# Finishing output tiles one by one, folding the last gate into the weights, and running the last accumulators in one stretch each, in a fused S4-convolution and SwiGLU block

## The chip, the cores and the metric

The kernel runs on one core of a Trainium2 chip. Each core has TensorE (PE, matrix multiply, writes only to PSUM banks), VectorE (DVE), ScalarE (ACT) and GpSimd (POOL), and DMA queues fed by the sync engine (SP) and others. Each engine takes its own queue of instructions in order and waits on semaphores for the others. The metric is the device time of one execution in microseconds (us), lower is better.

## The reference

One block of an adaptive-layer-norm network on 2048 tokens of 640 channels. The first half (a layer norm, a diagonal state-space convolution, a gate) leaves the stream `x`; the second half, which is all that the change touches, is:

```
h = layernorm(x) * (1 + cb) + sb              # cb, sb, gb: 640 values each, from c @ w_mod
out = (silu(h @ w1) * (h @ w3)) @ w2          # w1, w3: 640 x 1728; w2: 1728 x 640
x = x + gb * out
```

## The kernel before

All matrix products are made in three passes of a reduced-precision format: an operand is split into a high part (a cast on ScalarE) and a low part (operand minus high part, on VectorE), and each product is high x high, high x low, low x high. The tiles of high and low parts are named `gh`, `gl` (weights), `uh`, `ul` (the other weights, or the hidden values `h`), `xA`, `xB`, `T1` to `T4` (the normalised stream). Each of these pairs has two buffers, a raw weight `rw` has five.

The tokens are cut into four **quarters** of 512, worked in two **pairs** (A and B). A pair goes through three parts:

- A few hidden slices of 128 channels (`simple`) are made plainly (`plain`): for A, then for B, 15 matmuls for each of the two projections.
- The other slices (`rest`) go through `seven`, a Strassen-like scheme that makes A and B together with seven products in place of eight. It needs differences of the two quarters, `T1` to `T4`, made by `x_sums` (differences, two on VectorE and two on GpSimd) and `x_sum_split` (split in high and low). Each block of `seven` is 54 matmuls. It takes one PSUM bank of the three of `psG` for `b1` and one for `b4`.
- `outputs` multiplies the hidden values by `w2` and adds to the stream. It takes the 14 slices for quarter A (`c` is 0) and then for quarter B (`c` is 1), 28 steps `n`, 15 matmuls each: accumulators `acc[0]` to `acc[3]` hold 128 tokens by 512 channels, `acc[4]` holds the last 128 channels of all 512 tokens transposed. `operands(n + 1)` splits the next step's weight and hidden slice.

When a quarter's 14 steps are over, ScalarE scales `acc[4]` by the gate into `ob`, VectorE multiplies each `acc[k]` by the gate row `gbr` into `gated[k]`, four PE transposes (`tail`, into one bank of `psG`) turn `ob` back, VectorE adds the four transposed pieces and the four gated pieces to the stream tiles `xr`, and four DMAs (`x_out`) store them. For three of the four quarters this is `rest_of`, done in one go after the next step (or, at the change of pairs, after the next pair's plain slices); for the last quarter it is done as the accumulators end.

While pair 0 is in `outputs`, `prepare` makes the stream of pair 1 as side work of the steps: loads, layer norm, transposes (`turn_a`, `turn_b`), then `x_sums` and `x_sum_split` of the tiles in steps 21 to 27.

The order on each engine is the program's order inside `outputs` (it sets `in_order`); elsewhere a scheduler orders the instructions, and `tc.issue_after(ins)` (and `behind(...)`, which wraps it for several instructions) keeps what is written in it behind `ins` on the engine of `ins`. Through a helper, nearly every operation from here on has line L102 in the profile, so tiles tell them apart.

Of the kernel before, what the change touches and what calls it, by code (L numbers as in the profile page):

```python
# [13 lines left out]
OP = mybir.AluOpType  # L14
# [3 lines left out]
P = 128  # L18
# [12 lines left out]
NFT = 14  # L31
# [76 lines left out]
def tile_kernel(ctx: ExitStack, tc: tile.TileContext, a):  # L108
# [780 lines left out]
    def bank(g):  # L889
        return psG.tile([P, 512], F32, name="ps", tag="g") if g else psA.tile([P, 512], F32, name="ps", tag="acc")  # L890

    def room(i):

        return wq.tile([P, 512], F32, name=f"s{i}")
# [327 lines left out]
    def x_out(j, x):  # L1222
        SQ.dma_start(a["out"][j * P:(j + 1) * P, :], x)

    def outputs(q0, order, hs, side, last):


        seq = [(c, f) for c in range(2) for f in order]
        n_all, raws, ops, xr, accs, late = len(seq), {}, {}, [], [], []

        def load(n):
            if n < n_all:
                raws[n] = weight(seq[n][1], "w2")

        def operands(n):
            if n < n_all:
                c, f = seq[n]
                ops[n] = out_operands(raws.pop(n), hs[c][f], f)

        def tail(q, ob, x):  # L1240

            pt = bank(1)
            for i in range(4):
                PE.transpose(pt[:, i * P:(i + 1) * P], ob[:, i * P:(i + 1) * P], ident)
            for i in range(4):
                V.tensor_tensor(x[i][:, 512:], pt[:, i * P:(i + 1) * P], x[i][:, 512:], op=OP.add)

        in_order[0] = True
        for n in range(5):
            load(n)  # L1250
        operands(0)
        in_order[0] = False
        yield
        in_order[0] = True
        for n, (c, f) in enumerate(seq):
            q, pos = q0 + c, n % NFT
            operands(n + 1)
            load(n + 5)
            if pos == 10:
                xr = [x_tile(), x_tile()] + ([x_tile(), x_tile()] if c or last else [x_place("T41"), x_place("T31")])  # L1260
                for i in range(4):
                    SQ.dma_start(xr[i], xs[4 * q + i])
            if pos == 0:
                acc = {k: bank(0) for k in (4, 0, 1, 2, 3)}
            side(n)
            terms = ops.pop(n)

            if c and last and pos == NFT - 2:
                held = terms
                continue  # L1270
            if c and last and pos == NFT - 1:
                terms = held + terms
            if pos == NFT - 1:
                if last or c == 0:
                    gated = [room(4 + i) for i in range(4)]
                else:
                    gated = places(3) + places(3)[:1]
            for k in (4, 0, 1, 2, 3):
                for i, (hh, w) in enumerate(terms):
                    lhs, rhs = (hh[:, k * P:(k + 1) * P], w[:, :512]) if k < 4 else (w[:, 512:], hh)  # L1280
                    PE.matmul(acc[k], lhs, rhs, start=(pos == 0 and i == 0),
                              stop=(pos == NFT - 1 and i == len(terms) - 1))
                if pos < NFT - 1:
                    continue

                if k == 4:
                    ob = room(8)
                    S.activation(ob, acc[4], AF.Copy, scale=modT[:, 2, 4:5])
                    continue
                V.tensor_tensor(gated[k], acc[k], gbr, op=OP.mult)  # L1290
                if c == 0 or not last:
                    continue
                if k == 0:
                    tail(q, ob, xr)
                V.tensor_tensor(xr[k][:, :512], gated[k], xr[k][:, :512], op=OP.add)
                x_out(4 * q + k, xr[k])
            for t in late:
                t()
            late = []
            if pos == NFT - 1 and not (c and last):  # L1300
                def rest_of(q=q, ob=ob, x=xr, gated=gated):
                    tail(q, ob, x)
                    for i in range(4):
                        V.tensor_tensor(x[i][:, :512], gated[i], x[i][:, :512], op=OP.add)
                        x_out(4 * q + i, x[i])
                late.append(rest_of)
        side(n_all)
        in_order[0] = False
        yield
        for t in late:  # L1310
            t()

    def prepare(q0, g):


        steps, got, tiles = {}, {}, ([], [])

        def at(n, fn):
            steps.setdefault(n, []).append(fn)

        mids = (3, 5, 7, 9, 11, 13, 15, 17)
        for i, n in enumerate(mids):
            at(n + 2, lambda i=i: x_norm(4 * q0 + i, got[i], tiles[i // 4], got[i][0]))
        both = []

        def get(i, place):
            if i < 4:
                x = x_next[i]
            elif i < 6:
                x = x_place(("T40", "T21")[i - 4])  # L1330
            else:
                both.extend(places(1) if i == 6 else ())
                x = both[0][:, i - 6]
            got[i] = x_get(4 * q0 + i, x, i < 4, z_place(place) if place else None)

        for i, (n, place) in enumerate(((0, "xB23"), (1, "T120"), (3, "xA01"), (5, "xA23"), (6, "xB23"), (8, "T120"),
                                        (10, None), (12, None))):
            at(n, lambda i=i, place=place: get(i, place))
        for k, n in enumerate((12, 12, 14, 14, 16)):
            at(n, lambda k=k: turn_a(q0, tiles[0], k, g))  # L1340
        for k, n in zip((4, 0, 2, 3, 1), (20, 20, 21, 22, 23)):
            at(n, lambda k=k: turn_b(q0 + 1, tiles[1], k, g))
        for i, n in enumerate(mids):
            at(n, lambda i=i: x_mid(4 * q0 + i, got[i], g))
        for n, i, p in ((21, 0, 0), (22, 0, 1), (23, 0, 2), (24, 0, 3), (24, 1, 0), (24, 1, 1), (25, 1, 2), (26, 1, 3)):
            at(n, lambda i=i, p=p: x_sums(i, (p,)))
        for n, i, name in ((22, 0, "T1"), (24, 0, "T2"), (26, 1, "T1")):
            at(n, lambda i=i, name=name: x_sum_split(i, (name,)))
        at(24, lambda: fetch(NFT - 1, "wg"))
        at(26, lambda: first_block.append(blocks(0)))  # L1350
        at(27, lambda: first_plain.append(plain_weights(NFT - 1)))
        at(27, lambda: x_sum_split(1, ("T2",)))
        at(27, lambda: w_sums(first_block[0], range(4)))
        at(28, lambda: w_split(first_block[0], (1, 0, 2, 3)))

        def side(n):
            for fn in steps.get(n, ()):
                fn()
        return side

    def places(n):

        t = tz.tile([P, SD, 3, NA], F32, name="A").rearrange("p k s b -> p (k s b)")
        if n == 1:
            return [t[:, :2 * D].rearrange("p (i d) -> p i d", i=2)]
        return [t[:, i * 512:(i + 1) * 512] for i in range(3)]

    last_f = NFT - 1
    output = iter(())
    x_next, first_block, first_plain = [], [], []  # L1370
    for pair in range(2):
# [40 lines left out]
        for n, f in enumerate(simple[::-1]):  # L1412
            hB[f] = h_tile()
            ws = ws or plain_weights(f)
            plain("B", f, hB[f], ws)
            ws = None
            if pair == 0 and n < 2:
                x_sums(n)
                x_sum_split(n)
        for i in range(2):  # L1420
            x_late(i)
        if pair:
            for i in range(2):
                x_sum_split(i, ("T4",))
        next(output, None)
        free = []
        order = rest[:10] + ([0, last_f, 1, 2] if pair == 0 else [last_f] + rest[10:])
        output = outputs(q0, order, (hA, hB), prepare(q0 + 2, 1) if pair == 0 else lambda n: None, pair == 1)
        if first_block:
# [8 lines left out]
        for n, f in enumerate(rest):  # L1438
            nxt = block_split(blocks(rest[n + 1])) if n + 1 < len(rest) else None
            if n < 12:  # L1440
                free = free or places(3)
                hA[f] = free.pop(0)
            else:
                hA[f] = h_tile()
            hB[f] = h_tile()
            if pair == 0 and n == len(rest) - 4:
                x_next += [x_tile() for _ in range(4)]
                with tc.issue_after(loaded[0].ins):
                    for i in range(4):
                        SQ.dma_start(x_next[i], a["x"][(8 + i) * P:(9 + i) * P, :])  # L1450
            if nxt is None:
                next(output)
            end = seven(W, hA[f], hB[f], nxt)
            W = nxt
        next(output)
    next(output, None)
# [51 lines left out]
```

## Time and profile before

| | us |
|---|---|
| median of three runs (lowest, highest) | 996.03 (994.35, 996.17) |
| profiled execution, its own time | 997.93 |
| span of the profiled execution, first to last instruction | 995.3 |
| PE busy in the span | 922.2 |
| VectorE, ScalarE, GpSimd busy | 698.1, 541.2, 266.7 |

The second half of the block takes the span from about 427 us on. The profiled execution is 1.9 us above the median of the runs. A row of the profile's timeline gives the start, the time, the engine, the line, the operation, the tile written and the tiles read, the sizes, the number of instructions merged, and in brackets how long the engine was idle ahead of it and who released it.

### The profile page before, as it was taken

How to read it: one execution, taken by the hardware profiler on the slowest of the kernel's cores; microseconds unless marked ns; L12 is line 12 of the kernel's file. 1: busy time of each engine (PE TensorE's matmuls, PEld its weight loads, DVE VectorE, ACT ScalarE, POOL GpSimd, SP SyncE). 2: the span in 40 equal slices, each digit the busy share in tenths (PEclk: the TensorE clock that was granted, in tenths of full speed). 3: DMA queues.
4: the chain of work that ended last, by engine and by line, in shares of the span. 5: the costliest groups of instructions: out<-in, count | busy, mean ns of one | idle time of the engine just before them, and what ended most of it. 6: DMA issues, size and time to landing. Idle time of an engine off the chain costs nothing.

```text
span 995.3 us, 20571 instructions
## 1 busy us (share of the span) xinstructions
PE 922.2 (93%) x8214; PEld 689.2 (69%) x8214; DVE 698.1 (70%) x1243; ACT 541.2 (54%) x793; POOL 266.7 (27%) x274
## 2 busy tenths in 40 slices
PE   5898797998988889799999999999989999999997
PEld 2545354666666666467888888777768888888876
DVE  5598856888898886667666665577876666654545
ACT  3658665899999973246433333365633333333432
POOL 1553333544444530214422210111422222200000
PEclk9855777999999999899999999999989999999999
DMA  9463586554566687785313113995431111213452
GB/s 272 158 228 114 200 198 188 150 150 121 148 161 155 166 211 226 222 183 216 93 54 106 54 53 93 240 263 172 133 119 53 54 54 54 55 38 93 145 165 100
DMA packets 103571, 140.74 MB, mean 141 GB/s; under 512 B 20564, under 2 KB 62676, under 8 KB 103476
## 3 DMA queue, kind: packets, MB, share of 16 engines
q1 hardware_dynamic: 99668, 129.34, 45.2%
q0 software_dynamic: 2304, 7.74, 2.3%
q10 hardware_dynamic: 1504, 2.36, 0.9%
q8 instruction: 64, 1.05, 0.5%
q14 instruction: 31, 0.25, 0.1%
HBM read 107.94 MB, written 31.46 MB: 140 GB/s over the span
## 4 chain that ended last, share of the span: by engine, by line
PE 66%; ACT 14%; DVE 10%; DMA 3%; issue 3%; POOL 2%; SPq 1%; ACTq 0%; POOLq 0%; DVEq 0%
PE ps L102 51%; ACT cs L135 4%; ACT A L135 3%; ACT ph L135 3%; PE p L570 2%; PE pa L432 2%; ACT L135 2%; PE pq L444 2%; PE pt L539 1%; POOL ph L472 1%; PE pm L299 1%; DMA zs<-zt 1%; PE pu L406 1%; PE pk L521 1%; PE pz L612 1%
## 5 line engine op out<-in xcount | busy, mean ns | idle before, releaser
L102 DVE TENSOR_TENSOR s<-ps,s 128x512 f32<-128x512 f32 x138 | 94.8, 688 | 86.3 <-PE ps L102 84.5
L472 POOL TENSOR_TENSOR ph<-thi,iota 128x1024 int32<-128x1024 int32 x40 | 85.5, 2136 | 175.1 <-DVE A L508 78.2
L102 DVE TENSOR_TENSOR gl<-rw,gh 128x640 fp32r<-128x640 f32 x87 | 77.7, 893 | 72.3 <-ACT gh L102 72.3
L102 ACT CAST gh<-rw 128x640 fp32r<-128x640 f32 x87 | 63.3, 727 | 103.8 <-PE ps L102 87.9
L102 PE MATMUL ps<-xA,gh 128*128 128x512 f32 x280 | 89.0, 397 | 4.4 <-DVE h L102 4.1
L570 PE MATMUL p<-uk,s 128*64 128x256 f32 x640 | 79.1, 389 | 14.0 <-PE pa L432 5.6
L102 PE MATMUL ps<-gh,uh 128*128 128x512 f32 x224 | 87.5, 391 | 0.0
L102 PE MATMUL ps<-gl,uh 128*128 128x512 f32 x224 | 87.2, 389 | 0.0
L102 POOL TENSOR_TENSOR S<-rw 128x256 f32<-128x256 f32 x46 | 37.0, 806 | 180.3 <-DVE S0l L102 148.0
L102 PE MATMUL ps<-gh,ul 128*128 128x512 f32 x208 | 81.1, 390 | 0.0
L570 PEld LDWEIGHTS p<-uk,s 128*64 128x64 f32 x640 | 45.2, 138 | 39.3 <-PE pa L432 8.4
L102 PEld LDWEIGHTS ps<-xA,gh 128*128 128x128 f32 x280 | 53.3, 191 | 17.6 <-DVE h L102 4.5
L102 PE MATMUL ps<-xA,gl 128*128 128x512 f32 x140 | 55.2, 394 | 0.0
L135 ACT ACTIVATE A<-pa 128x1024 f32<-128x1024 f32 x40 | 40.4, 1024 | 25.7 <-PE pa L432 24.4
L497 DVE TENSOR_TENSOR E<-A,cs 128x1024 f32<-128x1024 f32 x40 | 51.1, 1277 | 1.7 <-ACT A L135 1.7
L504 DVE TENSOR_TENSOR A<-A,ph 128x1024 f32<-128x1024 f32 x40 | 50.2, 1255 | 0.0
L102 ACT ACTIVATE s<-ps 128x512 f32<-128x512 f32 (+1 forms) x33 | 19.7, 597 | 54.1 <-PE ps L102 49.3
L612 PE MATMUL pz<-Y,i 64*128 64x128 f32 x640 | 45.1, 285 | 4.1 <-issue 2.8
L612 PEld LDWEIGHTS pz<-Y,i 64*128 64x128 f32 x640 | 38.9, 189 | 13.9 <-issue 11.2
L102 PEld LDWEIGHTS ps<-gl,uh 128*128 128x128 f32 x224 | 42.1, 188 | 9.0
L102 PEld LDWEIGHTS ps<-gh,uh 128*128 128x128 f32 x224 | 42.1, 188 | 8.7
L539 PE MATMUL pt<-s,K 128*64 128x128 f32 x640 | 47.3, 291 | 0.5 <-ACT uk L138 0.5
(259 smaller groups left out, 2332.8 us busy)
## 6 DMA issues: line engine op xcount, KB each, us to landing
rw<-in_w_dram SPq DMA_DIRECT2D x52, 320.0 KB
us<-u SPq DMA_DIRECT2D x16, 640.0 KB
s<-in_s_dram SPq DMA_DIRECT2D x40, 256.0 KB
i<-in_i_dram SPq DMA_DIRECT2D x40, 256.0 KB
rw<-in_wg_dram SPq DMA_DIRECT2D x31, 320.0 KB
rw<-in_wu_dram SPq DMA_DIRECT2D x28, 320.0 KB
uk<-us SPq DMA_DIRECT2D x32, 256.0 KB
zs<-zt SPq DMA_DIRECT2D x32, 256.0 KB
```

The source lines that it names most:

```text
L102: ins = fn(*args, **kw)
L135: return tc.keep_in_program_order(S.activation(*args, **kw))
L299: PE.matmul(pm[g, :n], scb[:, k], w[:, k, :], start=(k < 4), stop=(k > 0), tile_position=(0, g.start))
L406: PE.matmul(pu[h][hh * 64:hh * 64 + 64, q, :320], s1r[r], x[r, hh * 320:hh * 320 + 320], start=not (one and h == 0), stop=True, tile_posit ...
L432: keep(PE.matmul(pA[s][:, rr, :], w[r, ch, :], r2[r, js, :].rearrange("p j b -> p (j b)"), start=st, stop=not st, tile_position=(r.start, 0)))
L444: keep(PE.matmul(pQ[s][:, rr, :256], w[r, ch, :], rv, start=(i == 0), stop=(i == 3), tile_position=(r.start, 0)))
L472: hold(G.tensor_tensor(p, bc(thi[:, sl], 2, NPH), bc(iota, 1, SD), op=OP.mult))
L497: keep(V.tensor_tensor(EC[s][:, :, 1:3, :], AA[s][:, :, 1:3, :], mid(cs[s]), op=OP.mult))
L504: keep(V.tensor_tensor(A[:, :, 1:3, :], A[:, :, 1:3, :], mid(ph[s]), op=OP.mult))
L539: keep(PE.matmul(pt[c * 64:c * 64 + 64, g, :], kk[:, g, :], s1[:, c, :], start=True, stop=True, tile_position=(0, c * 64)))
L570: keep(PE.matmul(p2[par * 64:par * 64 + 64, pi, c, :], s2[:, pi * 2 + par, c * 64:c * 64 + 64], uk[:, 0:kn + 1:kn, f, :], start=True, stop ...
L612: ins = keep(PE.matmul(pz[:, par, (g % 2) * 2 + pi, :], i1[r, pi, c, :], Y[r, pi, c, :], start=(c == 0), stop=(c == 1), tile_position=(par ...
```

## The change

1. **Tile by tile.** `rest_of` is replaced by four steps `finish`, one for each tile of 128 tokens: one PE transpose into a bank of its own, the add of the transposed piece, the add of the gated piece, the store. Inside `outputs` two are done after each of the next two steps. At the change of pairs they are done one each behind blocks 1 to 4 of the next pair's `seven`, through `before` (the old generator, which now yields after each), and `ob` moves from `room(8)`, which `plain` also uses, to one of the `places`.
2. **Last gate in the weights.** In the last quarter `gate` multiplies the first 512 columns of each of its 14 raw `w2` tiles by `gbr` on VectorE, two steps ahead of their split. The four gate multiplies at the end fall away, and the accumulators are added to the stream straight from PSUM.
3. **Last accumulators in one run each.** Of the last two steps only `acc[2]` and `acc[3]` are held back; the step before the last runs `acc[4]`, `acc[0]`, `acc[1]` with its own operands. The four tails come after `acc[1]`, in four banks.
4. **`T2` behind the change of pairs.** The split of `T2` is taken out of steps 24 and 27 and written after the plain slices of pair 1.
5. In pair 0, `x_sums` and `x_sum_split` are put `behind(*turned)`, the last splits of the plain `xA`/`xB` tiles.

```
+        def gate(n):
+
+            if last and NFT <= n < n_all:
+                V.tensor_tensor(raws[n][:, :512], raws[n][:, :512], gbr, op=OP.mult)
+
...
-        def tail(q, ob, x):
-
-            pt = bank(1)
-            for i in range(4):
-                PE.transpose(pt[:, i * P:(i + 1) * P], ob[:, i * P:(i + 1) * P], ident)
-            for i in range(4):
-                V.tensor_tensor(x[i][:, 512:], pt[:, i * P:(i + 1) * P], x[i][:, 512:], op=OP.add)
+        def tail(i, ob, x, g):
+
+            pt = bank(g)
+            PE.transpose(pt[:, :P], ob[:, i * P:(i + 1) * P], ident)
+            V.tensor_tensor(x[i][:, 512:], pt[:, :P], x[i][:, 512:], op=OP.add)
+
+        def finish(i, q, ob, x, gated, g):
+
+            tail(i, ob, x, g)
+            V.tensor_tensor(x[i][:, :512], gated[i], x[i][:, :512], op=OP.add)
+            x_out(4 * q + i, x[i])
...
             operands(n + 1)
             load(n + 5)
+            gate(n + 3)
...
             terms = ops.pop(n)
+            run = [(k, terms) for k in (4, 0, 1, 2, 3)]
 
             if c and last and pos == NFT - 2:
-                held = terms
-                continue
+                held, run = terms, run[:3]
             if c and last and pos == NFT - 1:
-                terms = held + terms
+                run[3:] = [(k, held + terms) for k in (2, 3)]
             if pos == NFT - 1:
-                if last or c == 0:
-                    gated = [room(4 + i) for i in range(4)]
+                if c == 0:
+                    gated, ob = [room(4 + i) for i in range(4)], room(8)
+                elif last:
+                    ob = room(8)
                 else:
-                    gated = places(3) + places(3)[:1]
-            for k in (4, 0, 1, 2, 3):
+                    *gated, ob = places(3) + places(3)[:2]
+            for k, terms in run:
...
-                V.tensor_tensor(gated[k], acc[k], gbr, op=OP.mult)
-                if c == 0 or not last:
-                    continue
-                if k == 0:
-                    tail(q, ob, xr)
-                V.tensor_tensor(xr[k][:, :512], gated[k], xr[k][:, :512], op=OP.add)
-                x_out(4 * q + k, xr[k])
-            for t in late:
+                elif not (c and last):
+                    V.tensor_tensor(gated[k], acc[k], gbr, op=OP.mult)
+                else:
+                    V.tensor_tensor(xr[k][:, :512], acc[k], xr[k][:, :512], op=OP.add)
+                    if k == 1:
+                        for i in range(4):
+                            tail(i, ob, xr, 1)
+                    for i in ((), (0, 1), (2,), (3,))[k]:
+                        x_out(4 * q + i, xr[i])
+            for t in late[:2]:
                 t()
-            late = []
+            late = late[2:]
             if pos == NFT - 1 and not (c and last):
...
+                late = [lambda i=i, t=(q, ob, xr, gated, 1 - c): finish(i, *t) for i in range(4)]
...
-        for n, i, name in ((22, 0, "T1"), (24, 0, "T2"), (26, 1, "T1")):
+        for n, i, name in ((22, 0, "T1"), (26, 1, "T1")):
...
-        at(27, lambda: x_sum_split(1, ("T2",)))
...
             if pair == 0 and n < 2:
-                x_sums(n)
-                x_sum_split(n)
+                with behind(*turned):
+                    x_sums(n)
+                    x_sum_split(n)
+        if pair:
+            for i in range(2):
+                x_sum_split(i, ("T2",))
...
-        next(output, None)
-        free = []
+        before, free = output, []
...
             end = seven(W, hA[f], hB[f], nxt)
+            if 1 <= n <= 4:
+                with behind(end):
+                    next(before, None)
```

How the built programs stand follows at three places. VectorE, ahead of pair 1's plain slices (`T_8157`, `T_8158` are `T1` of the second tile, `T_8183`, `T_8272` its `T2`, `T_8282`, `T_8284` its `T4`; the `gl` is the weight of the plain slice, `A<-ps,gbr` the gate multiplies of the quarter that has just ended). Before:

```order
L102 TENSOR_TENSOR ul<-h,uh 128x512
L102 TENSOR_TENSOR T_8157<-s_7607,T_8157 128x512
L102 TENSOR_TENSOR T_8282<-s_7715,T_8282 128x512
L102 TENSOR_TENSOR gl<-rw,gh 128x640
L102 TENSOR_TENSOR T_8183<-s_8034,T_8183 128x512
L102 TENSOR_TENSOR A<-ps,gbr 128x512 x4
```

The same place, with the change:

```order
L102 TENSOR_TENSOR ul<-h,uh 128x512
L102 TENSOR_TENSOR T_8158<-s_7607,T_8158 128x512
L102 TENSOR_TENSOR T_8272<-s_8037,T_8272 128x512
L102 TENSOR_TENSOR T_8284<-s_7715,T_8284 128x512
L102 TENSOR_TENSOR ul<-rw,uh 128x384
L102 TENSOR_TENSOR gl<-rw,gh 128x640
L102 TENSOR_TENSOR A<-ps,gbr 128x512 x4
```

The split of `T2` and a split of the first block's weight (`ul<-rw,uh 128x384`) now stand ahead of the plain slice's `gl`, where one split stood behind it and the other much later.

VectorE, from there to the first block of `seven` (`xm` are the stream tiles of the quarter that has ended, `h<-ps,s` 64x512 the plain slices' results for A and B, `T_8273`, `T_8276`, `T_8275`, `T_8278` the tiles `T3`, `s_8326` the first sum of the first block). Before:

```order
L102 TENSOR_TENSOR S3l<-S_8198,S3h 128x256
L102 TENSOR_TENSOR xm<-A,xm 128x512 x4
L102 TENSOR_TENSOR gl<-rw,gh 128x640
L102 TENSOR_TENSOR T_8273<-s_7963,T_8273 128x512
L102 TENSOR_TENSOR ul<-rw,uh 128x384 x2
L102 TENSOR_TENSOR xm<-ps,xm 128x128 x3
L102 TENSOR_TENSOR T_8276<-s_8070,T_8276 128x512
L102 TENSOR_TENSOR h<-ps,s_8250 64x512
L102 TENSOR_TENSOR xm<-ps,xm 128x128
L102 TENSOR_TENSOR gl<-rw,gh 128x640
L102 TENSOR_TENSOR h<-ps,s_8270 64x512
```

With the change:

```order
L102 TENSOR_TENSOR S3l<-S_8196,S3h 128x256
L102 TENSOR_TENSOR gl<-rw,gh 128x640
L102 TENSOR_TENSOR ul<-rw,uh 128x384
L102 TENSOR_TENSOR xm<-A,xm 128x512
L102 TENSOR_TENSOR h<-ps,s_8247 64x512
L102 TENSOR_TENSOR xm<-A,xm 128x512 x2
L102 TENSOR_TENSOR T_8275<-s_7966,T_8275 128x512
L102 TENSOR_TENSOR xm<-A,xm 128x512
L102 TENSOR_TENSOR gl<-rw,gh 128x640
L102 TENSOR_TENSOR h<-ps,s_8267 64x512
L102 TENSOR_TENSOR T_8278<-s_8073,T_8278 128x512
L102 TENSOR_TENSOR s_8326<-ps,s_8318 128x512
```

The weight's `gl` and `ul` moved ahead of the stream adds, both `h` moved forward, and the four adds `xm<-ps` are gone from here; the four adds `xm<-A` are still here.

PE, at the end (`ps_10133`, `ps_10134` are `acc[0]`, `acc[1]` before; `ps_10143`, `ps_10144` are `acc[1]`, `acc[2]` with the change; `ident` marks the transposes). Before:

```order
L102 MATMUL ps_10133<-gh_10442,uh_10446 128x512
L102 MATMUL ps_10133<-gl_10443,uh_10446 128x512
L102 MATMUL ps_10133<-gh_10442,ul_10447 128x512
L102 MATMUL ps_10469<-ident_63,s8_10460 128x128 x4
L102 MATMUL ps_10134<-gh_10419,uh_10423 128x512
L102 MATMUL ps_10134<-gl_10420,uh_10423 128x512
L102 MATMUL ps_10134<-gh_10419,ul_10424 128x512
```

With the change:

```order
L102 MATMUL ps_10143<-gh_10464,uh_10468 128x512
L102 MATMUL ps_10143<-gl_10465,uh_10468 128x512
L102 MATMUL ps_10143<-gh_10464,ul_10469 128x512
L102 MATMUL ps_10494<-ident_63,s8_10481 128x128
L102 MATMUL ps_10497<-ident_63,s8_10481 128x128
L102 MATMUL ps_10500<-ident_63,s8_10481 128x128
L102 MATMUL ps_10503<-ident_63,s8_10481 128x128
L102 MATMUL ps_10144<-gh_10441,uh_10445 128x512
L102 MATMUL ps_10144<-gl_10442,uh_10445 128x512
L102 MATMUL ps_10144<-gh_10441,ul_10446 128x512
```

The transposes moved from behind `acc[0]` to behind `acc[1]`, and write four banks of a pool that has three buffers, where they wrote one.

More of the change, by code (lines that the diff above doesn't have):

```diff
@@ L1286, in outputs @@
                 if k == 4:
-                    ob = room(8)
                     S.activation(ob, acc[4], AF.Copy, scale=modT[:, 2, 4:5])
-                    continue
-                V.tensor_tensor(gated[k], acc[k], gbr, op=OP.mult)
-                if c == 0 or not last:
-                    continue
-                if k == 0:
-                    tail(q, ob, xr)
-                V.tensor_tensor(xr[k][:, :512], gated[k], xr[k][:, :512], op=OP.add)
-                x_out(4 * q + k, xr[k])
-            for t in late:
+                elif not (c and last):
[8 more added lines that the diff above has]
+            for t in late[:2]:
                 t()
-            late = []
+            late = late[2:]
             if pos == NFT - 1 and not (c and last):
[L1301 to L1306, printed above, removed]
+                late = [lambda i=i, t=(q, ob, xr, gated, 1 - c): finish(i, *t) for i in range(4)]
         side(n_all)
@@ L1311, in outputs @@
             t()
+            yield
     def prepare(q0, g):
```

## The prediction

> **What bounds the kernel now.** I read the page first, then busy times by stage, then the timeline of each engine wherever PE pauses behind 427 us.
>
> ```profile
> span 995.3 us, 20571 instructions
> 725.00:750.00 25.00, 20.94 (x83) 16.82 (x82) 19.06 (x32) 8.24 (x16) 6.90 (x8) 0.86 0.37 120
> 975.00:1000.00 25.00, 14.89 (x65) 11.35 (x63) 10.45 (x19) 4.44 (x7) 0.00 (x0) 0.89 0.14 53
> ```
>
> A stage row gives the stretch, its length, PE's busy time, then those of the others; the last but two is the granted clock. From 475 to 975 us only this one row in 25 us falls well below 25 us of PE, and it is at the change of pairs, with a lower clock. PE is the bound, so an edit is worth what it takes out of PE's pauses, plus what it takes off the end.
>
> The change of pairs on PE and on VectorE:
>
> ```profile
> 721.10 0.39 PE L102 MATMUL ps<-xA,gl 128*128 128x512 f32 x1
> ...
> 729.97 0.40 PE L102 MATMUL ps<-T,S0h 128*128 128x512 f32 x1
> 734.43 1.22 PE L102 MATMUL ps<-xA,gh 128*128 128x512 f32 x2 [4.06 <-DVE h L102]
> ...
> 740.10 0.63 PE L102 MATMUL ps<-xA,gh 128*128 128x512 f32 x2
> ...
> 747.15 0.62 PE L102 MATMUL ps<-xA,gh 128*128 128x512 f32 x2
> ...
> 748.51 0.62 PE L102 MATMUL ps<-T,S1h 128*128 128x512 f32 x2
> ```
>
> ```profile
> 717.05 2.38 DVE L102 TENSOR_TENSOR T<-s,T 128x512 fp32r<-128x512 f32 x2
> 719.35 1.36 DVE L102 TENSOR_TENSOR gl<-rw,gh 128x640 fp32r<-128x640 f32 x1
> 720.63 1.22 DVE L102 TENSOR_TENSOR T<-s,T 128x512 fp32r<-128x512 f32 x1
> 721.77 2.47 DVE L102 TENSOR_TENSOR A<-ps,gbr 128x512 f32<-128x512 f32 x4
> ...
> 726.05 4.12 DVE L102 TENSOR_TENSOR xm<-A,xm 128x512 f32<-128x512 f32 x4
> 730.10 0.81 DVE L102 TENSOR_TENSOR gl<-rw,gh 128x640 fp32r<-128x640 f32 x1
> ...
> 732.37 0.67 DVE L102 TENSOR_TENSOR xm<-ps,xm 128x128 f32<-128x128 f32 x3
> ...
> 733.68 0.69 DVE L102 TENSOR_TENSOR h<-ps,s 64x512 f32<-64x512 f32 x1
> ```
>
> Six matmuls go from 747.15 to 748.51, so 0.227 each. PE stands still from 730.2 to 734.43 (4.2 us): its next matmul needs a bank that `h` (733.68) frees, and `h` stands behind the stream adds. Then 13 matmuls take 5.67 us (734.43 to 740.10) in place of 2.95: the clock is halved, 2.7 more. With 0.2 of switching to and from the transposes the place costs 7.1 us.
>
> The other pauses:
>
> ```profile
> 467.59 0.39 PE L102 MATMUL ps<-xB,gh 128*128 128x512 f32 x1
> 468.65 0.50 PE L102 MATMUL ps<-xB,gh 128*128 128x512 f32 x1 [0.68 <-DVE xB L102]
> ```
>
> ```profile
> 466.75 1.30 POOL L102 TENSOR_TENSOR s<-s,s 128x512 f32<-128x512 f32 x1 [1.43 <-DVE s L102]
> ```
>
> ```profile
> 467.19 1.40 DVE L102 TENSOR_TENSOR xB<-s,xB 128x512 fp32r<-128x512 f32 x1
> ```
>
> ```profile
> 712.40 0.39 PE L102 MATMUL ps<-uh,gh 128*128 128x512 f32 x1
> 713.54 0.49 PE L102 MATMUL ps<-uh,gl 128*128 128x512 f32 x1 [0.76 <-DVE gl L102]
> 714.15 0.50 PE L102 MATMUL ps<-ul,gh 128*128 128x512 f32 x1
> ```
>
> ```profile
> 707.69 1.32 DVE L102 TENSOR_TENSOR gl<-rw,gh 128x640 fp32r<-128x640 f32 x1 [0.74 <-ACT gh L102]
> ...
> 710.37 2.38 DVE L102 TENSOR_TENSOR T<-s,T 128x512 fp32r<-128x512 f32 x2
> 712.68 0.81 DVE L102 TENSOR_TENSOR gl<-rw,gh 128x640 fp32r<-128x640 f32 x1
> ```
>
> ```profile
> 947.78 0.39 PE L102 MATMUL ps<-uh,gh 128*128 128x512 f32 x1
> 948.62 0.50 PE L102 MATMUL ps<-uh,gl 128*128 128x512 f32 x1 [0.44 <-DVE gl L102]
> 949.22 0.50 PE L102 MATMUL ps<-ul,gh 128*128 128x512 f32 x1
> ```
>
> ```profile
> 982.22 0.39 PE L102 MATMUL ps<-ul,gh 128*128 128x512 f32 x1
> 983.26 0.50 PE L102 MATMUL ps<-uh,gh 128*128 128x512 f32 x1 [0.66 <-ACT uh L102]
> ...
> 985.93 0.60 PE L102 MATMUL ps<-ident,s 128*128 128x128 f32 x4
> ```
>
> Less 0.227 per matmul started, they cost: at 467, 1.06 - 0.23 = 0.8 (0.9 with the slower next); at 712, 1.75 - 0.45 = 1.3; at 947, 1.44 - 0.45 = 1.0; at 982, 10 matmuls take 3.71 in place of 2.27, so 1.4.
>
> **The change, part by part.**
>
> *Change of pairs.* VectorE's queue decides, and it is walked in the new order. An f32 128x512 operation takes 0.60 when nothing runs on GpSimd (2.47 for four) and 1.0 to 1.2 beside it (2.38 for two, 4.12 for four). One `T2` split, 1.2, leaves the queue ahead of 712.68 (it goes ahead of the weight split of 707.69, into its 0.74 of idle time), so the `gl` there comes 1.0 sooner and of the 1.3 at 712 some 0.3 is left. Ahead of the plain `gl` of 719.35 there now stand the other `T2` split (1.2) and a `ul` of 384 columns (estimate 0.8, 384/512 of 1.1). The four `A` adds then start at 721.77 - 1.2 + 0.8 = 721.4, and the plain `gl`, now last ahead of them, ends there; PE wanted it at 721.10 - 1.0 = 720.1 and waits 1.3. Plain A and B end 28 matmuls later, 727.8. The next weight's `gl` stands at the end of the small splits (726.05 - 0.4 = 725.7) and is done at 726.9, in time. With the tails gone, `b1` has the third bank free: no wait where 4.2 us stood. Then `ul` 0.7, one `xm` 1.0, `h` of A at 729.2; ScalarE needs that for B's silu, then copies `b1` at about 730.9, and PE, which wanted to go on with `b1` 12 matmuls after 727.8 (730.5), waits 0.4. VectorE goes on with two `xm`, `T3`, `xm`, `gl`, `h` of B, `T3` and the first sum, eight at 0.6 to 0.7: 734.2, and PE wants that sum at 730.9 + 15 x 0.227 = 734.3. [...] The other 27 matmuls of the block end at 740.5, where before it was 747.15: **-6.6**. Bounds: -7.4, all waits gone; -2.5, if VectorE is 1.4 later and the clock drops again (2.7).
>
> [...]
>
> [...]
>
> *Tails in blocks 1 to 4.* One transpose each, alone between matmuls of 512. A merged row of four takes 0.35 to the next matmul, so one alone is bounded by 0.1 and 0.35; I take 0.25, nearer the top since the switch is paid each time: **+1.0** (0.4 to 1.4). VectorE has room there. Each store now stands in SP's queue between two weight loads and waits for VectorE's add, so the load behind it waits too; in the program's order the first one comes behind the loads for block 5, whose buffers come free only then, and a weight is loaded two blocks (24 us) early: 0.
>
> *First boundary, 671 us.* Here `prepare` takes two banks of the same pool right behind the transposes.
>
> ```profile
> 670.69 0.60 PE L102 MATMUL ps<-ident,s 128*128 128x128 f32 x4
> ```
>
> ```profile
> 671.33 0.49 DVE L102 TENSOR_TENSOR xm<-ps,xm 128x128 f32<-128x128 f32 x2
> ```
>
> With two banks for two tails, its second bank is the first tail's, free when VectorE has added it: 671.33 + 0.3 = 671.65. PE wants it at about 671.05: **+0.5** (0 to 0.9).
>
> *Pair 0, 467 us.* The differences go behind the last `xB` split, so GpSimd's 1.30 no longer lies beside it, and the split ends 0.9 sooner: **-0.9** (-0.95 to 0). The weight split pushed behind them (`gl` for the third plain slice) is wanted some 11 us later than 468.65, and its queue needs about 9. GpSimd's four differences start 4.5 us later, at about 468.5, but without the gaps between them; they end no later than now, and so do the weight sums behind them.
>
> *Third quarter, 947 us.* The `gl` stood behind four stream adds, 0.6 each; two of these now stand a step later, with two of the stores, which hold up SP's next weight load by a step of the five that it is ahead: **-1.0** (-1.1 to -0.3).
>
> *Gate in the weights.* 14 multiplies of 128x512 on VectorE, 0.6 to 0.7 each, 9 us in all, on a VectorE that idles ahead of each weight split:
>
> ```profile
> L102 DVE TENSOR_TENSOR gl<-rw,gh 128x640 fp32r<-128x640 f32 x28 | 23.1, 824 | 43.1 <-ACT gh L102 43.1
> ```
>
> 43.1/28 is 1.5 us per step, and GpSimd is idle: cost 0. If that cover were gone, 0.7 for each step.
>
> *The end.*
>
> ```profile
> 986.12 0.69 DVE L102 TENSOR_TENSOR s<-ps,gbr 128x512 f32<-128x512 f32 x1 [1.98 <-PE ps L102]
> ...
> 991.50 0.69 DVE L102 TENSOR_TENSOR xm<-s,xm 128x512 f32<-128x512 f32 x1
> ```
>
> From the first matmul of the last-but-one step (two ahead of 982.22, 981.76) PE now does 9, then 3, 3, 3 of the last step, with no wait, since the last hidden split is ready at 983.2: `acc[1]` is done at 985.8. Three transposes, then the fourth waits for a bank, so for VectorE: `xr[0]`, `xr[1]` to 986.65, first tail to 986.95. PE goes on at 987.1 with 12 matmuls to 989.8, and the last add (0.4 behind the last matmul's start, as 986.12 is behind its own) runs from 990.05 to 990.75, where it now ends at 992.2. The last store follows as before (995.3 - 992.2 = 3.1): **-1.4**, of which the bank costs 0.8 (bounds -2.3 to -0.7).
>
> Sum: -6.6 + 1.0 + 0.5 - 0.9 - 1.0 - 1.4 = **-8.4 us**. On the profiled execution's 997.93 that is 989.5; it lies 1.9 above the median, as runs of a kernel differ by about that, so on the median 996.03 it gives **987.6**.
>
> **The rivals.**
>
> *VectorE stays late at the change of pairs.* The four adds `xm<-A` still stand there, and two splits more stand ahead of plain A. [...] For it speaks the queue without a gap from 714 to 734; against it, that `h` of A is 4.5 us sooner.
>
> *All waits go.* The fourth transpose and the `gl` of plain A are not waited for (0.8 + 1.3 + 0.4): 985.1. Against it, a pool of three buffers.
>
> *The gate holds VectorE.* Each multiply waits for its weight's load, in order, with `gl` of the next step behind it. VectorE has 1.5 - 0.7 = 0.8 us to spare a step, so a load late by 1.4 us costs 0.6 x 14 = 8.4, all of the gain, and one late by 2.2 gives 1007. Against it: a raw weight has five buffers and is loaded some three steps (10 us) ahead of its gate, and the last store's 3.1 us is the price of one such transfer.
>
> *It does not do what it says.* The scheduler leaves the stream adds in place and PE waits as long: only the end and the quarters pay, 994.2.
>
> **How the numbers follow.** Forecast 0.66, late VectorE 0.16, all waits go 0.08, nothing at the change of pairs 0.06, the gate 0.04. Faster by over 0.2% (2 us, about what a measurement here can tell): 0.66 + 0.16 + 0.08 and a little of the fourth, 0.91; same 0.05; slower 0.04. The range is 985.0 to 991.8: it takes in the forecast's bounds one or two at a time and the first two rivals.
>
> **What would show it.** PE has no pause over 2 us from 720 to 745 and no clock of 0.5 there; a pause of about 1 us on `gl` stands near 720; none near 467 and 947; the fourth transpose at the end waits about 0.8 for VectorE. A halved clock behind 720, or `gh` waiting for VectorE's gate step after step in the last quarter, would make it wrong.

## The result and the profile after

| | before | after |
|---|---|---|
| median of 7 runs of each, us | 996.17 | 991.21 |
| ratio, 95% interval | | 0.9947 (0.9926 to 0.9967) |
| profiled execution: time, span, us | 997.93, 995.3 | 991.21, 989.4 |

The change makes the kernel 5.0 us faster where 8.4 were forecast: the sign was right, the size was not, and the time lies near the upper end of the range that was given, 985.0 to 991.8. Single executions of the changed kernel took from 986.72 to 993.36 us, so the terms are read as lengths of stages within one trace. A stage goes from one PE row to another that both kernels have. Of the executions of the changed kernel that y2 timed, one took 1735.49 us; it is left out of the median given there.

Stage rows of the changed kernel, columns as in the prediction's first fence:

```profile
span 989.4 us, 20588 instructions
475.00:500.00 25.00, 23.62 (x103) 18.95 (x102) 18.03 (x28) 10.72 (x21) 9.81 (x11) 1.00 0.31 93
725.00:750.00 25.00, 24.25 (x107) 19.73 (x106) 20.61 (x34) 9.53 (x18) 6.90 (x8) 1.00 0.24 76
```

From 725 to 750 PE is busy 24.25 us where it was 20.94, and the granted clock is 1.00 where it was 0.86. A stage that was full before, 475 to 500, has lost 1.4 us of PE: a new pause.

The change of pairs on PE, first the row of before that opens it, then the changed kernel:

```profile
703.07 0.38 PE L102 MATMUL ps<-ident,A 128*128 128x128 f32 x2
```

```profile
703.90 0.38 PE L102 MATMUL ps<-ident,A 128*128 128x128 f32 x2
...
721.45 0.61 PE L102 MATMUL ps<-xA,gh 128*128 128x512 f32 x2
723.20 0.50 PE L102 MATMUL ps<-xA,gl 128*128 128x512 f32 x1 [1.13 <-DVE gl L102]
...
732.17 0.39 PE L102 MATMUL ps<-T,S1l 128*128 128x512 f32 x1
733.31 0.74 PE L102 MATMUL ps<-xA,gh 128*128 128x512 f32 x2 [0.75 <-ACT s L102]
...
744.37 0.62 PE L102 MATMUL ps<-T,S1h 128*128 128x512 f32 x2
```

From the last transposes of the output stage to the first `S1h` of the second block it was 748.51 - 703.07 = 45.44 us; now it is 744.37 - 703.90 = 40.47: **-4.97**. Two pauses stand there, 1.30 for the plain `gl` (721.45, two matmuls of 0.227 taken off) and 0.91 for ScalarE's copy of `b1` (732.17). Ahead of them the `gl` at 712 to 715 still costs 0.99, and a new 0.36 stands at 710.7: PE waits there for VectorE's split of a hidden slice (710.48), and the split of `T2` (708.48, behind its cast on ScalarE) now stands ahead of that.

The `gl` at 712 was to come 1.0 sooner. On VectorE and on GpSimd:

```profile
712.41 1.91 DVE L102 TENSOR_TENSOR gl<-rw,gh 128x640 fp32r<-128x640 f32 x1
```

```profile
712.03 1.60 POOL L102 TENSOR_TENSOR s<-s,s 128x512 f32<-128x512 f32 x1 [2.87 <-ACT gh L102]
```

It took 1.91 beside GpSimd's difference, where it took 0.81 before, and so ended 10.42 behind the row that opens the stage (714.32 - 703.90), exactly as before (713.49 - 703.07).

The new pause in pair 0, on PE, then on VectorE, then on GpSimd:

```profile
478.17 0.39 PE L102 MATMUL ps<-T,ul 128*128 128x512 f32 x1
478.80 0.73 PE L102 MATMUL ps<-xB,gh 128*128 128x512 f32 x2 [0.24 <-DVE h L102]
480.67 0.50 PE L102 MATMUL ps<-xB,gl 128*128 128x512 f32 x1 [1.14 <-DVE gl L102]
```

```profile
471.77 1.77 DVE L102 TENSOR_TENSOR s<-s,s 128x512 f32<-128x512 f32 x1
473.46 4.68 DVE L102 TENSOR_TENSOR T<-s,T 128x512 fp32r<-128x512 f32 x4
...
479.27 1.35 DVE L102 TENSOR_TENSOR gl<-rw,gh 128x640 fp32r<-128x640 f32 x1
```

```profile
471.32 1.67 POOL L102 TENSOR_TENSOR s<-s,s 128x512 f32<-128x512 f32 x1 [0.63 <-DVE s L102]
473.62 1.68 POOL L102 TENSOR_TENSOR s<-s,s 128x512 f32<-128x512 f32 x1 [0.63 <-DVE s L102]
```

The pause of 0.94 at 467 is gone; this one costs 0.40 + 1.42 + 0.11 = 1.93.

A tail ahead of the second block and the end, on PE:

```profile
755.25 0.27 PE L102 MATMUL ps<-ident,A 128*128 128x128 f32 x1
755.28 0.71 PE L102 MATMUL ps<-xA,gh 128*128 128x512 f32 x2
755.82 0.39 PE L102 MATMUL ps<-xA,gl 128*128 128x512 f32 x1
```

```profile
981.30 0.49 PE L102 MATMUL ps<-ident,s 128*128 128x128 f32 x3
982.45 0.33 PE L102 MATMUL ps<-ident,s 128*128 128x128 f32 x1 [0.65 <-DVE xm L102]
```

From the tail's transpose to the third matmul behind it is 0.57, for two matmuls of 0.227: 0.12 lost. At the end the fourth transpose follows 1.15 behind the row of three; with 0.057 taken off for each of the three, a quarter of a matmul's 0.227 and so an estimate, 0.98 is lost. The three themselves start 0.11 apart (0.49 for three, 0.27 for one); by that it is 0.82.

| stage | before, us | after, us | forecast | measured |
|---|---|---|---|---|
| pair 0, 459.87 and 459.12 to 666.40 and 666.62 | 206.53 | 207.50 | -0.9 | +0.97 |
| first boundary, from there to 703.07 and 703.90 | 36.67 | 37.28 | +0.5 | +0.61 |
| change of pairs | 45.44 | 40.47 | -6.6 | -4.97 |
| four blocks with tails (12.24 each; 748.51 to 797.47, 744.37 to 793.91) | 48.96 | 49.54 | +1.0 | +0.58 |
| third quarter's tail, from there to 976.10 and 971.44 | 178.63 | 177.53 | -1.0 | -1.10 |
| end, from there to the span's end | 19.2 | 17.96 | -1.4 | -1.24 |

The six sum to -5.15. The two spans differ by 5.9, of which 0.75 lies ahead of 459 us, where the change touches nothing; the medians differ by 5.0. Two terms fail: pair 0 by 1.9 with the wrong sign, and the change of pairs by 1.6.

### The profile page after: what moved, and what is told of

Read it like the earlier page. It is cut to its first block, busy times and chain, and to the rows that moved or that the text cites. A ratio compares the mean times of both kernels' runs of the same rounds, so it can differ in the third digit from the quotient of the medians.

```text
span 989.4 us, 20588 instructions
## 1 busy us (share of the span) xinstructions
PE 918.2 (93%) x8214; PEld 686.2 (69%) x8214; DVE 706.2 (71%) x1253; ACT 540.9 (55%) x793; POOL 265.5 (27%) x274
## 3 DMA queue, kind: packets, MB, share of 16 engines
q8 instruction: 64, 1.05, 0.4%
## 4 chain that ended last, share of the span: by engine, by line
PE 65%; ACT 16%; DVE 10%; DMA 3%; issue 3%; POOL 2%; SPq 0%; ACTq 0%; DVEq 0%; POOLq 0%
PE ps L102 50%; ACT cs L135 4%; ACT A L135 3%; ACT ph L135 3%; PE p L570 2%; PE pa L432 2%; ACT L135 2%; PE pq L444 2%; DMA zs<-zt 2%; PE pt L539 1%; PE pm L299 1%; PE pk L521 1%; PE pz L612 1%; PE pu L406 1%; POOL ph L472 1%
```

## The experiments

Each of x1 to x8 was executed once, with its trace, so their stages are compared and not their whole times. Parts 1 and 3 of the change were not undone by themselves: what they are worth is read from the stages above alone.

### x1 and x2: each wait at the change of pairs by itself

x1 undoes the part on `T2` alone:

```diff
-        for n, i, name in ((22, 0, "T1"), (26, 1, "T1")):
+        for n, i, name in ((22, 0, "T1"), (24, 0, "T2"), (26, 1, "T1")):
...
+        at(27, lambda: x_sum_split(1, ("T2",)))
...
-        if pair:
-            for i in range(2):
-                x_sum_split(i, ("T2",))
```

> Only the part on T2 is undone: its two splits stand in steps 24 and 27 of the output stage again, everything else as in the changed kernel. Theory 1 (the two splits and the 384-column ul ahead of the plain gl are what PE waits for at 721): the plain gl ends 2.2 us sooner, so the pause of 1.30 there is gone (under 0.2), so is the 0.36 at 710.7, where a T2 cast stands ahead of gh on ScalarE, and the pause at 712 to 715 grows from 0.99 back to the 1.3 of before; the second block of the last pair then starts about 1.3 us sooner against the start of the step at 704. Theory 2, that of the prediction (the move is worth 1.0 at 712 and costs nothing else): the block starts 0.3 to 1.0 later, with 1.3 at 712 and some pause still at 721.

```profile
700.96 0.38 PE L102 MATMUL ps<-ident,A 128*128 128x128 f32 x2
...
727.82 0.39 PE L102 MATMUL ps<-T,S1l 128*128 128x512 f32 x1
729.77 0.73 PE L102 MATMUL ps<-xA,gh 128*128 128x512 f32 x2 [1.56 <-ACT s L102]
...
733.77 0.74 PE L102 MATMUL ps<-xB,uh 128*128 128x512 f32 x2 [0.30 <-DVE s L102]
...
741.43 0.61 PE L102 MATMUL ps<-T,S1h 128*128 128x512 f32 x2
```

The waits went as theory 1 has it (none at 721, 0.36 gone at 710, 1.39 at 712), but the stage takes 741.43 - 700.96 = 40.47 us, the same as with the part in. The 1.3 of `gl` came back as 0.8 more for the copy of `b1` and 0.46 for VectorE's sum. Neither theory's number holds: this part of the change is worth nothing in this kernel. With the `T2` split back in its queue the `gl` at 712 ends 10.42 behind the row that opens the stage (711.38 - 700.96), the same as without it.

x2 makes two edits far apart:

```diff
-        sg = room(8)
+        sg = h if last and c == "B" else room(8)
...
-                            tail(i, ob, xr, 1)
+                            tail(i, ob, xr, int(i < 3))
```

> Two edits 250 us apart, read from the trace apart. (a) The silu of plain B of the 64-row slice is written into B's own h tile, so that it needn't wait until VectorE has read A's silu out of the common buffer. If that wait is the cause of the 0.91 at 732 (ScalarE's copy of b1 stands behind the silu, the silu behind h of A), the pause is gone and the second block of the last pair starts 0.9 sooner. If ScalarE is late for another reason, the copy of b1 starts within 0.3 of where it did and the pause stays over 0.5. (b) The fourth transpose at the end takes the bank that acc[4] left, in place of the third bank of the transposes. If the bank is the cause of its wait for VectorE (0.98), the wait is gone and the span ends 0.8 to 1.0 sooner behind the fourth transpose; if VectorE is the bound at the end, the last add starts within 0.3 of where it did against the start of the last step.

```profile
736.43 0.39 PE L102 MATMUL ps<-T,S0l 128*128 128x512 f32 x1
737.58 0.73 PE L102 MATMUL ps<-xB,uh 128*128 128x512 f32 x2 [0.76 <-DVE s L102]
...
982.16 0.60 PE L102 MATMUL ps<-ident,s 128*128 128x128 f32 x4
```

(a) The pause at 732 is gone, and 0.92 stands at 736.43 for VectorE's sum instead; the stage is 40.44. The cause named for the pause was right, its removal bought nothing. (b) The four transposes run in one row, and from there to the end of the span it takes 989.3 - 982.16 = 7.1 us where it was 8.1: the bank was the wait, about 0.9 (spans are given to 0.1).

### x5 to x8: VectorE's queue, and both chains at once

x5 keeps the four `xm<-A` adds out of the change of pairs (a), and puts the gate back on the outputs of the last quarter (b):

```diff
-        V.tensor_tensor(hA, c21, sg, op=OP.mult)
+        vend[0] = V.tensor_tensor(hA, c21, sg, op=OP.mult)
...
-                with behind(end):
+                with behind(end, vend[0]):
                     next(before, None)
...
-                V.tensor_tensor(raws[n][:, :512], raws[n][:, :512], gbr, op=OP.mult)
...
-                    V.tensor_tensor(xr[k][:, :512], acc[k], xr[k][:, :512], op=OP.add)
+                    V.tensor_tensor(gated[k], acc[k], gbr, op=OP.mult)
+                    V.tensor_tensor(xr[k][:, :512], gated[k], xr[k][:, :512], op=OP.add)
```

> Two edits 170 us apart, read apart. (a) The tails of blocks 1 to 4 go behind the last VectorE instruction of their block too, not only behind its last matmul: the four 512-column adds xm<-A that VectorE works off at 729 to 734, in the change of pairs, come behind blocks 1 to 4. Two runs so far moved the waits there (T2 back in the steps; a place of its own for B's silu) and won nothing. Theory 1: VectorE's whole queue from 714 to 737 is the bound. Without the four adds (3.1 us of it) the pauses at 732 and 736 together are under 0.3, the pause of 1.3 at the plain gl stays, since the adds stand behind it, and block 1 starts 0.9 to 1.0 sooner against the step at 704. Theory 2: ScalarE's chain of silu and copy is the bound, the adds only fill gaps: a pause of 0.6 or more stays at 732 to 737. (b) The gate goes back from the weights to the outputs in the last quarter (14 multiplies less in the steps, four more at the end). If the gate in the weights costs nothing, the steps from 907 to 971 take as long as before within 0.2; if it costs, they are shorter. The end is 1.2 to 1.8 later: two more multiplies ahead of the tails, one ahead of the last add.

VectorE in the changed kernel, and then in x5, from the weight splits to the first sum:

```profile
727.34 1.36 DVE L102 TENSOR_TENSOR gl<-rw,gh 128x640 fp32r<-128x640 f32 x1
728.63 1.09 DVE L102 TENSOR_TENSOR ul<-rw,uh 128x384 fp32r<-128x384 f32 x1
729.64 1.22 DVE L102 TENSOR_TENSOR xm<-A,xm 128x512 f32<-128x512 f32 x1
730.89 0.69 DVE L102 TENSOR_TENSOR h<-ps,s 64x512 f32<-64x512 f32 x1
731.51 1.28 DVE L102 TENSOR_TENSOR xm<-A,xm 128x512 f32<-128x512 f32 x2
...
733.31 0.68 DVE L102 TENSOR_TENSOR xm<-A,xm 128x512 f32<-128x512 f32 x1
...
735.97 0.69 DVE L102 TENSOR_TENSOR s<-ps,s 128x512 f32<-128x512 f32 x1
```

```profile
726.95 1.09 DVE L102 TENSOR_TENSOR ul<-rw,uh 128x384 fp32r<-128x384 f32 x1
728.07 0.69 DVE L102 TENSOR_TENSOR h<-ps,s 64x512 f32<-64x512 f32 x1
...
731.34 0.69 DVE L102 TENSOR_TENSOR s<-ps,s 128x512 f32<-128x512 f32 x1
...
734.34 0.69 DVE L102 TENSOR_TENSOR s<-ps,s 128x512 f32<-128x512 f32 x1 [1.98 <-PE ps L102]
```

(a) From `ul` to the first sum it is 7.34 us with the adds, 4.39 without. No pause is left at 732, nor at 736, where x2 had one; 1.3 is left at the plain `gl`, and the stage takes 39.39: 1.08 less, as theory 1 has it. VectorE then even idles 1.98 behind the first sum.

(b) From the first step of the last pair's output stage to the last transposes the changed kernel takes 981.30 - 890.48 = 90.82 us, x5 978.52 - 887.74 = 90.78: the gate in the weights costs nothing. The end is 10.2 long in place of 8.1, 2.1 later, above the 1.2 to 1.8 expected: the fourth transpose alone waits 1.4 more.

x6 is (a) of x5 with x1; x7 adds x2's two edits and takes the differences of pair 0 out of `behind(*turned)`; x8 is x7 without x1's edit.

```diff
-                with behind(*turned):
-                    x_sums(n)
-                    x_sum_split(n)
+                x_sums(n)
+                x_sum_split(n)
```

> The four xm<-A adds behind blocks 1 to 4 as in the run x5, and the T2 splits back in steps 24 and 27 as in x1, gate as in the changed kernel. Theory 1 (VectorE's queue as a whole is the bound, and with 3.1 us out of it the splits find room): no pause over 0.3 at 721, 732 or 736, 1.3 stays at 712; block 1 starts 2.0 to 2.4 sooner than in the changed kernel against the step at 704. Theory 2 (each wait is of its own chain, T2's cost comes back behind 727 whatever else stands there): 0.9 to 1.2 sooner, with a pause of about 1 at 728.

> x6 with B's silu in its own place, the fourth bank at the end, and the differences of pair 0 no longer held behind the last xB split. By the terms measured apart, against the changed kernel: 2.0 to 2.4 at the change of pairs, 0.9 at the end, 1.0 at 467 to 480 (the pause of 0.94 at 467 returns, the 1.9 at 478 goes): 3.9 to 4.3 sooner from 434 to the end. If the terms are not independent, the sum falls short by more than 0.5.

> x7 without the T2 splits back in the steps: behind the change of pairs as in the changed kernel. If the adds alone free the change of pairs, 0.9 to 1.0 there, with the plain gl's 1.3 left; with 0.9 at the end and 1.0 at 467 to 480, 2.8 to 3.0 sooner than the changed kernel from 434 to the end, so 1.0 to 1.4 later than x7.

PE in x6, ScalarE in x6, and the stage row of x7:

```profile
729.85 0.39 PE L102 MATMUL ps<-T,S1l 128*128 128x512 f32 x1
731.80 0.74 PE L102 MATMUL ps<-xA,gh 128*128 128x512 f32 x2 [1.56 <-ACT s L102]
```

```profile
730.17 0.59 ACT L102 ACTIVATE s<-ps 64x512 f32<-64x512 f32 x1 [2.11 <-DVE h L102]
...
731.17 0.58 ACT L102 COPY s<-ps 128x512 f32<-128x512 f32 x1
```

```profile
725.00:750.00 25.00, 25.00 (x111) 20.57 (x110) 19.61 (x33) 10.14 (x21) 8.83 (x11) 1.00 0.27 80
```

| | T2 back | B's silu apart | adds late | change of pairs, us |
|---|---|---|---|---|
| changed kernel | | | | 40.47 |
| x1 | yes | | | 40.47 |
| x2 | | yes | | 40.44 |
| x5 | | | yes | 39.39 |
| x6 | yes | | yes | 39.83 |
| x8 | | yes | yes | 39.38 |
| x7 | yes | yes | yes | 38.05 |

x6 is nearer theory 2, but has neither theory's number: 1.72 for the copy of `b1`, with 0.64 won in place of 2.0 to 2.4 or 0.9 to 1.2. There ScalarE's silu of B waits 2.11 for A's `h`, which reads the buffer it writes. x7 has none of the pauses behind 715 left and takes 2.42 off. So two chains end within a microsecond of each other in the first block: the buffer of the silu (A's `h`, B's silu, the copy of `b1`) and VectorE's queue up to the first sum. T2 back is worth 0, -0.4 or 1.3 us, by which of the two it still finds. The eighth combination, T2 back and the silu apart with the adds in place, was not run.

Over all stages x7 gains 2.42 + 0.91 (pair 0, 206.59) + 0.89 (end) = 4.2 on the changed kernel, x8 1.09 + 0.96 + 0.9 = 2.9, both as expected: the terms of different stages add up, those of one stage don't.

### x3: the weights ahead of the differences

```diff
-            ws = None
+            ws = plain_weights(simple[::-1][n + 1]) if pair == 0 and n < 3 and n > 0 else None
             if pair == 0 and n < 2:
                 with behind(*turned):
```

> The differences stay behind the last xB split, but the third plain slice's weights are split ahead of the second pair of differences in the program's order; VectorE's gl there now stands ahead of three T splits and a difference instead of behind them. Theory 1 (the new pause of 1.9 us at 478 is the place of gl in VectorE's queue, behind splits that wait for GpSimd's differences): no pause over 0.3 from 465 to 485, so the stage up to 640 us is 1.7 to 2.0 shorter than in the changed kernel, and 0.9 shorter than in the kernel before, as predicted. Theory 2 (VectorE and GpSimd hold each other up, so what is put later is late wherever gl stands): the pause moves on to ul, h or the first weight sums, and the stage gains less than 0.5.

On PE and on ScalarE:

```profile
482.60 0.39 PE L102 MATMUL ps<-T,gl 128*128 128x512 f32 x1
484.23 0.73 PE L102 MATMUL ps<-xB,gh 128*128 128x512 f32 x2 [1.23 <-ACT s L102]
```

```profile
482.65 0.41 ACT L102 CAST S3h<-S 128x256 fp32r<-128x256 f32 x1 [0.26 <-POOL S L102]
482.96 0.72 ACT L102 CAST gh<-rw 128x640 fp32r<-128x640 f32 x1
483.59 0.59 ACT L102 ACTIVATE s<-ps 128x512 f32<-128x512 f32 x1
```

No pause for `gl` is left, but 1.40 stands at 482.60: PE waits for a bank that a silu frees, the silu stands behind casts on ScalarE, and those wait for GpSimd's weight sums behind the last difference. The stage from 460 to 667 is 207.08, so 0.42 was won of 1.9: theory 2's size. Holding the differences for the sake of 0.9 us at 467 makes three engines late; x7, where they are not held, has 206.59, within 0.06 of the kernel before, with the old pause back.

### x4: what a pause does to the clock

```diff
-            V.tensor_tensor(h[1], hf, h[0].bitcast(F32), op=OP.subtract)
+            for _ in range(1 + again):
+                V.tensor_tensor(h[1], hf, h[0].bitcast(F32), op=OP.subtract)
...
-                ops[n] = out_operands(raws.pop(n), hs[c][f], f)
+                ops[n] = out_operands(raws.pop(n), hs[c][f], f, {3: 6, 5: 7, 7: 8, 9: 9}.get(n, 0) if last else 0)
```

> A measurement of what a pause does to the clock. In the third quarter VectorE repeats the split of h 6, 7, 8 and 9 times more ahead of four steps, at 0.60 each with about 1.25 us to spare, so that PE pauses for about 2.4, 3.0, 3.6 and 4.2 us, one pause in every second step. Theory 1 (the clock halves by the length of the pause, between the 1.3 that left it alone and the 4.06 that halved it): the step of 15 matmuls behind the shorter pauses takes 3.4 us as elsewhere, and the step behind the longer ones 2.5 to 3 us more. Theory 2 (the halving at the change of pairs came from that place, not from the length): none of the four steps takes more than 0.5 over 3.4, or all do.

PE at the second of the pauses:

```profile
912.72 0.39 PE L102 MATMUL ps<-uh,gl 128*128 128x512 f32 x1
916.62 0.50 PE L102 MATMUL ps<-ul,gh 128*128 128x512 f32 x1 [3.51 <-DVE ul L102]
```

Stage rows of x4 around the second pause:

```profile
904.40:908.00 3.60, 3.56 (x9) 2.84 (x10) 1.32 (x2) 0.00 (x0) 0.00 (x0) 0.53 0.30 91
...
916.60:918.10 1.50, 1.48 (x6) 1.24 (x7) 1.30 (x2) 0.00 (x0) 0.00 (x0) 0.99 0.00 0
918.10:921.50 3.40, 3.40 (x9) 2.67 (x8) 0.00 (x0) 0.12 (x1) 0.00 (x0) 0.50 0.34 96
921.50:924.90 3.40, 3.40 (x16) 2.82 (x15) 2.69 (x4) 1.13 (x2) 0.00 (x0) 1.00 0.25 65
```

All four pauses (2.94, 3.67, 4.27 and 5.08, longer than meant) were followed by a halved clock, the shortest too, so no length between 2.94 and 4.06 parts those that halve it from those that don't. Nor does the loss follow the length: behind the pauses 1.7, 1.7, 2.7 and 2.3 us were lost. Behind the second the clock is full for six matmuls, 916.62 to 918.1, and halves then.

The granted clock is 0.50 from 904.41 to 907.83, 918.07 to 921.48, 928.31 to 935.13 and 941.96 to 948.79. Each of these edges lies a whole number of times 3.41 us behind the first, so they keep a beat of 3.41 us here. Counted in spans of that length from edge to edge, with 0.227 of work for a matmul, 918.08 minus 3.41 to 918.08 holds 1.46 us of work (43%) and the next is halved; the span ahead of it holds 1.69 (49.5%) and the next is not. Behind the third and the fourth pause PE starts so late that the first halved span holds only five and three matmuls, 1.1 and 0.7 us, and the next is halved too; a span filled at half clock holds eight, 1.8 us (53%), and the clock is full behind it.

Theory 1 falls: the clock halved behind the shorter pauses too, and the loss does not follow the length. Theory 2 named "or all do", which is what came, but its reason, that the place of the change of pairs is special, falls, since this is another place. That the share of work in one span decides the clock of the next is the author's reading of these four pauses; no further run tested it.

### y1 and y2: timed

> The kernel of x7 again, timed in rounds beside the kernel before and the changed kernel on the same chip. From the stages of x7 against those of the changed kernel: 2.42 at the change of pairs, 0.91 from 460 to 666 us, 0.96 at the end, 4.3 in all, so with the changed kernel's 5.0 some 9.3 us under the kernel before, a ratio of 0.9907. If the stages' gains are given back elsewhere, the ratio is 0.993 or more.

> The changed kernel unaltered, on the same chip as y1: a ratio of 0.995 to the kernel before, as measured at first, and 4.3 us above y1.

x7's kernel: median 985.88 us, ratio to the kernel before 0.9898 (0.9876 to 0.9920). The changed kernel: 990.29, ratio 0.9937 (0.9916 to 0.9958). By the medians x7's edits are worth 4.4 us on the changed kernel, by the stages 4.2; the two intervals overlap by 0.0004. Both kernels are faster than the kernel before.

The two new traces also show how well a stage repeats. y1 has 206.55 and 38.06 us for pair 0 and the change of pairs, where x7 had 206.59 and 38.05. y2 has 207.51 and 40.50 where the changed kernel had 207.50 and 40.47, but 37.11 for the first boundary where it had 37.28.

## Why the prediction was right, and where not

- **Pair 0, forecast -0.9, measured +0.97: wrong.** The step "wanted some 11 us later than 468.65, and its queue needs about 9" failed. `gl` was wanted at about 479.3, as said. But the queue was priced as if GpSimd stood still: VectorE's two differences took 1.77 each and its four `T` splits 4.68 in place of 2.5. All but one of these six began while an operation of GpSimd was running and ended 0.55 behind the end of that one (473.54 behind 472.99, in the rows shown). The queue took until 480.6. The statement that GpSimd's sums end no later than before held within 0.3, and did not help. x7 and x8, which don't hold the differences, have 206.59 and 206.54 us, the kernel before 206.53: this part of the change is the cause.
- **Change of pairs, forecast -6.6, measured -4.97: mechanism right, size off.** No pause over 2 us and no halved clock (granted 1.00 from 420.14 to 990.16 us). The step "so the `gl` there comes 1.0 sooner" failed: the `gl` at 712 came no sooner, since GpSimd's difference now lay beside it. So 0.99 was left at 712 where 0.3 was forecast, with 0.36 at 710 that the walk left out. The other mis-sized term is the copy of `b1`: it was to wait 0.4, it waits 0.91 and another 0.13. That is 1.05 + 0.64, about the whole difference.
- **The 1.30 for the plain `gl`** came out as forecast by luck. Less the 0.83 by which the stage began later, PE wanted it at 721.1 and it ended at 722.3, where the walk had 720.1 and 721.4: both were about one us late.
- **The copy of `b1`.** The walk had `h` of A done at 729.2; it was done at 731.58, 1.5 late when the 0.83 is taken off. VectorE was 0.8 late when it began the four `A` adds (723.07 for 721.4), and `gl`, `ul` and one add, all beside GpSimd's sums, took 1.36, 1.09 and 1.22 where the walk had 1.2, 0.7 and 1.0.
- **VectorE beside GpSimd.** From 434 us on in the changed kernel, twelve 128x512 operations of VectorE with both inputs in SBUF began while one of GpSimd's was running (those of 128x1 left out), and eleven of them ended 0.55 us behind its end; the longest took 1.79, where the walk had 1.0 to 1.2. Another 21, which read PSUM, began so too and took 0.69 at most. This is behind both terms that failed. x5, which takes four two-input adds out of the queue, gained 1.08, but that is the adds' own time as well.
- **The rival "VectorE stays late"** was half of what happened: the adds do hold the queue (x5), but the clock did not halve; the longest pause was 1.30. With 4.0 less gain, 1.3 us more of waiting and the 2.7 of a halved clock, it comes to 991.6, the author's estimate: no run shows that 1.3 more would have halved the clock there. The measured 991.21 lies nearer this 991.6 than the forecast's 987.6, yet 1.9 of that distance is pair 0, which no rival named.
- **Tails in blocks 1 to 4:** 0.15 each (12.39 for a block in place of 12.24), where 0.25 was taken from between 0.1 and 0.35. The low end was nearer.
- **First boundary, +0.61 for +0.5; third quarter, -1.10 for -1.0; end, -1.24 for -1.4:** as worked out. x2 shows the bank's share at the end, about 0.9 for 0.8. Putting the last tail in another bank was there to be had.
- **Gate in the weights, 0:** x5 confirms it within 0.04 over 90.8 us.
- **Clock:** the forecast takes nothing for the clock behind the pauses that it leaves. That was the author's estimate; no run shows a length up to which a pause leaves the clock alone. For the 1.30 it held, the granted clock being 1.00 there. x4 has a pause of 2.94 us, shorter than the 4.06 of the kernel before, with 1.7 lost behind it. In the kernel before the clock was 0.50 from 733.21 to 740.04 us, 6.83, which agrees with the beat of 3.41 read off x4.

## What to carry to other kernels

Where one place has several waits, take them away together in one run before pricing each: x1 and x2 removed the waits that they aimed at and gained nothing, x7 removed all and gained 2.4 us. Price a queue by its instructions and by what the other engine does beside each of them: the one at 478 had two microseconds to spare on paper and none beside GpSimd. When an order is held back for the sake of one pause, follow the held work to every engine that it feeds, because the pause moves there.

## What the chip showed that was not expected

- In the changed kernel from 434 us on, a VectorE operation with both inputs in SBUF that began while GpSimd worked (128x1 operations left out) nearly always ended a fixed time behind GpSimd's operation, 0.55 us for 128x512 (eleven of twelve) and 0.68 for 128x640 (24 of 25), so its length was set by where GpSimd's ended: the `gl` at 712 took 1.91, where before it took 0.81 with GpSimd idle.
- A pause of 2.94 us was followed by a halved clock, as one of 5.08 was; the loss behind the pauses, 1.7 to 2.7 us, did not follow their length, and the edges of the halved clock lie whole numbers of times 3.41 us apart (x4).
- One transpose between matmuls of 512 costs 0.12 to 0.15 us on PE, less than half of the 0.35 that a merged row of four takes to the next matmul.
